# Four transformer layers on one core: the order and the queues of the first loads

## The chip, the cores and the metric

One Trainium2 chip, one core of it. The metric is the device time of one execution in microseconds (us). Profiles are one execution each, of the same programs; times in them count from the start of the span, which is about 1.8 us shorter than the device time.

## The reference

Input 2048 x 1024 in bf16; linear attention and a gated feed-forward layer, each with a layernorm ahead and a residual, two times over. Only the beginning matters here:

```python
x = A_x                                                        # 1 x 2048 x 1024
x = x + _A_ref(_layernorm(x, axis=-1), A_wqkv, A_wo)           # linear attention
x = x + _B_ref(_layernorm(x, axis=-1), B_W_gate, B_W_up, B_W_down)
...  # both once more
def _A_ref(x, wqkv, wo):
    q, k, v = ...(x @ wqkv)
    ...
```

Nothing can be multiplied before the first rows of x are loaded, normalized and transposed, and the first weights are there.

## The kernel before

Rows of x come in 16 blocks of 128 rows (256 KB each); weights in tiles of 1024 x 512 (1 MB). `k0`, `k1`, `q0`, `q1`, `v0` are such tiles of `wqkv`. The first four blocks make the first quarter. TensorE is kept busy with multiplications of zeros until block 0 is ready, for its clock.

```python
        for _ in range(11):
            nc.tensor.matmul(idle, lhsT=zero[:, 0:P], rhs=zero, start=True, stop=True)

        k0, k1, v0, q0, q1 = (ring.place() for _ in range(5))
        self.load_x(0, 0)                     # half of block 0, SyncE's queue
        self.load_x(0, 1, nc.scalar)          # other half, ScalarE's queue
        k0(0, H)
        self.load_x(1, None, nc.scalar)
        k0(H, 2 * H)
        self.load_x(2)
        k1()
        self.load_x(3)

        def load():
            for t in range(4, 8):
                self.load_x(t)
            q1()
            ...  # blocks 8 to 15 and v0, spread over later units
```

Then the units of work, in the order in which every engine gets them. A unit is the projection of one block with one weight tile: eight matmuls of 512 columns, 1.73 us at full clock.

```python
        def block0():
            stat(0, 0)
            stat(0, 1)
            rstd(0)
            stat(1, 0)                        # block 1's statistics, ahead of the scaling of block 0
            scale(0, 0)
            scale(0, 1)
            t0 = turn(0, 0)                   # transposes on TensorE
            t1 = turn(0, 1)
            t0("ss")
            stat(1, 1)
            rstd(1)
            q0(0, 2 * H, self.nc.scalar)      # query weights, ScalarE's queue
            t1("v")
            k(0, 0, between)
        ...
        return ([block0, block1, lambda: (turned(2), norm(3), k(0, 1)),
                 lambda: (turned(3), load(), k(1, 1)), lambda: q(0, 0), lambda: q(1, 0)]
                + ...)                        # k(2,0), k(2,1), q(2,0), k(3,0), ...
```

So the order on TensorE is k0 on blocks 0 and 1, k1 on blocks 0 and 1, then q0 on blocks 0 and 1. Blocks 2 and 3 are transposed by DMA on SyncE's queue.

Of the kernel before, what the change touches and what calls it, by code (L numbers as in the profile page):

```python
# [80 lines left out]
class _Net:  # L81
# [131 lines left out]
    def head(self):  # L213

        nc, tc, ring = self.nc, self.tc, self.ring
        H = self.KT // 2

        zero = self.ep.tile([P, NW], BF16, tag="e")
        nc.vector.memset(zero, 0.0)
        idle = self.ps3.tile([P, NW], F32, tag="b")  # L220
        for _ in range(11):
            nc.tensor.matmul(idle, lhsT=zero[:, 0:P], rhs=zero, start=True, stop=True)

        k0, k1, v0, q0, q1 = (ring.place() for _ in range(5))
        self.load_x(0, 0)
        self.load_x(0, 1, nc.scalar)
        k0(0, H)
        self.load_x(1, None, nc.scalar)
        k0(H, 2 * H)
        self.load_x(2)  # L230
        k1()
        self.load_x(3)

        def load():
            for t in range(4, 8):
                self.load_x(t)
            q1()
            for t in range(8, self.ST):
                self.later.at(3 + (t - 8) // 2 * 2, lambda t=t: self.load_x(t))
            self.later.at(11, v0)  # L240

        src = self.xb
        self.xnT[0, 0] = self.xnTp.tile([P, self.KT, QT * P], BF16, tag="xnT", name="xnT0_0")
        stats = [self.small.tile([P, 2, nc.vector.BN_STATS_DIM], F32, tag="stats", name=f"st{j}")
                 for j in range(QT)]
        rs, xn = {}, {}

        def stat(j, c):
            self.ln_stat(j, src[j], c, stats[j])

        def rstd(j):
            rs[j] = self.ln_rstd(stats[j])
            xn[j] = self.xn_home(0, j)

        def scale(j, h=None):
            self.ln_scale(src[j], *rs[j], xn[j], h)

        def turn(j, h):
            tp = self.ps3.tile([P, H, P], BF16, tag="b")
            for i in range(H):  # L260
                kt = h * H + i
                nc.tensor.transpose(tp[:, i, :], xn[j][:, kt * P:(kt + 1) * P], self.ident)  # L262
            dst = self.xnT[0, 0][:, h * H:(h + 1) * H, j * P:(j + 1) * P]

            def take(engine):
                if engine == "v":
                    nc.vector.tensor_copy(out=dst, in_=tp)
                elif engine == "s":
                    nc.scalar.activation(out=dst, in_=tp, func=ACT.Copy)
                else:  # L270
                    for i in range(0, H, 2):
                        nc.scalar.activation(out=dst[:, i:i + 2, :], in_=tp[:, i:i + 2, :],  # L272
                                             func=ACT.Copy)

            return take

        return load, q0, H, xn, stat, rstd, scale, turn

    def head_units(self, k, q, load, q0, H, xn, stat, rstd, scale, turn):

        def block0():
            stat(0, 0)
            stat(0, 1)
            rstd(0)
            stat(1, 0)
            scale(0, 0)
            scale(0, 1)
            t0 = turn(0, 0)
            t1 = turn(0, 1)
            t0("ss")  # L290
            stat(1, 1)
            rstd(1)
            q0(0, 2 * H, self.nc.scalar)
            t1("v")
            k(0, 0, between)

        def between():

            scale(1, 0)
            t0 = turn(1, 0)  # L300
            scale(1, 1)
            t0("v")

        def block1():
            turn(1, 1)("v")
            norm(2)
            k(1, 0)

        def norm(j):
            stat(j, 0)  # L310
            stat(j, 1)
            rstd(j)

        def turned(n):
            scale(n)
            self.ln_turn(0, n, xn[n])

        return ([block0, block1, lambda: (turned(2), norm(3), k(0, 1)),
                 lambda: (turned(3), load(), k(1, 1)), lambda: q(0, 0), lambda: q(1, 0)]
                + [lambda f=f, j=j, c=c: f(j, c) for j in (2, 3) for f, c in ((k, 0), (k, 1), (q, 0))]  # L320
                + [lambda j=j: q(j, 1) for j in range(QT)])
# [422 lines left out]
```

## Time and profile before

| what | us |
|---|---|
| median of 3 runs (lowest, highest) | 1627.52 (1626.98, 1627.64) |
| span of the profiled run | 1625.4 |
| TensorE busy | 1613.2 |
| first projection matmul starts | 7.49 |
| first query projection starts | 14.94 |
| last matmul of the program starts | 1622.12 |

The last two are starts of single matmuls in the trace. In the profile, "busy" of TensorE includes the matmuls' modelled ends, so a busy TensorE can still have lost some tenths of a us between two starts: the pauses below are taken from the distance of two starts, less the 0.216 us that is regular for 512 columns. The prediction shows the lines.

### The profile page before, as it was taken

How to read it: one execution, taken by the hardware profiler on the slowest of the kernel's cores; microseconds unless marked ns; L12 is line 12 of the kernel's file. 1: busy time of each engine (PE TensorE's matmuls, PEld its weight loads, DVE VectorE, ACT ScalarE, POOL GpSimd, SP SyncE). 2: the span in 40 equal slices, each digit the busy share in tenths (PEclk: the TensorE clock that was granted, in tenths of full speed). 3: DMA queues.
4: the chain of work that ended last, by engine and by line, in shares of the span. 5: the costliest groups of instructions: out<-in, count | busy, mean ns of one | idle time of the engine just before them, and what ended most of it. 6: DMA issues, size and time to landing. Idle time of an engine off the chain costs nothing.

```text
span 1625.4 us, 18607 instructions
## 1 busy us (share of the span) xinstructions
PE 1613.2 (99%) x7605; PEld 739.4 (45%) x7739; DVE 567.7 (35%) x940; ACT 330.4 (20%) x635; POOL 202.1 (12%) x134
## 2 busy tenths in 40 slices
PE   9999999999999999999999999999999999999999
PEld 4444444444444444444444444444444444444444
DVE  8844694113212222222264447932021112111211
ACT  6741212101110210111067312121011101101110
POOL 1449220000000000000023582100000000000000
PEclk9999999999999999999999999999999999999999
DMA  9314547447455545544550157464654455454442
GB/s 269 55 52 66 172 79 203 146 158 215 156 162 195 156 147 165 160 154 139 166 111 1 54 107 240 86 189 145 193 161 152 154 178 155 146 170 150 155 162 71
DMA packets 300358, 235.58 MB, mean 145 GB/s; under 512 B 103408, under 2 KB 296304, under 8 KB 300272
## 3 DMA queue, kind: packets, MB, share of 16 engines
q1 hardware_dynamic: 294192, 228.75, 48.3%
q10 hardware_dynamic: 6080, 5.64, 1.0%
q8 instruction: 60, 0.98, 0.3%
q14 instruction: 26, 0.21, 0.0%
HBM read 201.33 MB, written 8.39 MB: 129 GB/s over the span
## 4 chain that ended last, share of the span: by engine, by line
PE 99%; issue 0%; DMA 0%; DVE 0%; ACT 0%
PE pu L643 24%; PE pg L643 24%; PE acc L667 23%; PE ps L410 14%; PE ps L536 7%; PE ps L445 7%; PE kv L458 0%; PE acc_last L667 0%; DMA x<-in_A_x_dram 0%; PE fold L521 0%; PE tp L262 0%; PE ps L435 0%; ACT L692 0%; DVE xo L684 0%; DVE x L156 0%
## 5 line engine op out<-in xcount | busy, mean ns | idle before, releaser
L643 PEld LDWEIGHTS <-t 128*128 128x128 bf16 x3584 | 350.7, 98 | 422.8
L643 PE MATMUL pu<-xnT,t 128*128 128x512 bf16 x1756 | 420.1, 379 | 2.0
L643 PE MATMUL pg<-xnT,t 128*128 128x512 bf16 x1756 | 419.8, 379 | 1.8
L667 PE MATMUL acc<-t,hT 128*128 128x512 bf16 x1728 | 380.6, 379 | 1.9
L649 DVE TENSOR_TENSOR hT<-pu,rg 128x512 bf16<-128x512 f32 x224 | 154.8, 691 | 571.5 <-PE pu L643 555.0
L648 ACT ACTIVATE rg<-pg 128x512 f32<-128x512 f32 x224 | 133.5, 596 | 736.1 <-PE pg L643 661.7
L667 PEld LDWEIGHTS <-hT 128*128 128x128 bf16 x1820 | 178.1, 98 | 209.0
L410 PE MATMUL ps<-t,xnT 128*128 128x512 bf16 x1024 | 223.4, 379 | 0.2 <-ACT xnT L272 0.2
L410 PEld LDWEIGHTS <-xnT 128*128 128x128 bf16 x1024 | 99.4, 98 | 120.0 <-issue 1.5
L536 PE MATMUL ps<-T,pqT 128*128 128x512 bf16 x500 | 110.2, 379 | 0.6
L147 ACT ACTIVATE rstd<-mv,eps 128x1 f32<-128x1 f32 x64 | 18.8, 294 | 337.7 <-DVE mv L145 337.5
L684 DVE TENSOR_TENSOR xo<-x,acc 128x512 bf16<-128x512 f32 x31 | 21.3, 687 | 170.3 <-PE acc L667 169.5
L489 POOL TENSOR_TENSOR prod<-pq,zrow 128x1024 f32<-128x1024 bf16 x32 | 68.0, 2125 | 85.9 <-DVE den L494 72.4
L140 DVE BATCH_NORM_STATS2 stats<-x 128x6 f32<-128x512 f32 (+1 forms) x120 | 77.9, 671 | 1.2 <-DMA x<-in_A_x_dram 0.4
L536 PEld LDWEIGHTS <-pqT 128*128 128x128 bf16 x512 | 49.9, 98 | 60.4 <-issue 0.5
L425 POOL CAST ksum<-x 128x512 f32<-128x512 bf16 x2 | 1.7, 866 | 605.4 <-DVE x L361 605.4
L681 DVE TENSOR_TENSOR x<-x,acc 128x512 f32<-128x512 f32 x32 | 21.6, 674 | 138.5 <-PE acc L667 137.4
L427 POOL TENSOR_TENSOR ksum<-ksum,slab 128x512 f32<-128x512 f32 x46 | 54.1, 1183 | 80.3 <-DVE slab L361 63.0
L361 DVE SCALAR_TENSOR_TENSOR pq<-ps,e 128x512 bf16<-128x512 f32 x64 | 43.9, 686 | 53.3 <-ACT e L355 51.3
L501 POOL TENSOR_TENSOR pq<-pq,den 128x1024 bf16<-128x1024 bf16 x32 | 61.7, 1936 | 3.1 <-DVE den L496 3.1
L494 DVE TENSOR_REDUCE den<-prod 128x32 f32<-128x1024 f32 x32 | 38.9, 1217 | 54.0 <-POOL prod L489 54.0
L445 PE MATMUL ps<-slab,x 128*128 128x512 bf16 x249 | 55.7, 379 | 0.4
(57 smaller groups left out, 592.5 us busy)
## 6 DMA issues: line engine op xcount, KB each, us to landing
t<-in_B_W_gate_dram SPq DMA_DIRECT2D x56, 1024.0 KB, 7.3
t<-in_B_W_up_dram SPq DMA_DIRECT2D x56, 1024.0 KB, 5.4
t<-in_B_W_down_dram SPq DMA_DIRECT2D x64, 896.0 KB, 5.1
t<-in_A_wqkv_dram SPq DMA_DIRECT2D x10, 1024.0 KB, 5.1
t<-in_A_wo_dram SPq DMA_DIRECT2D x4, 1024.0 KB, 6.7
away<-x SPq DMA_DIRECT2D x8, 512.0 KB, 4.7
x<-away SPq DMA_DIRECT2D x8, 512.0 KB, 8.2
out_dram<-xo ACTq DMA_DIRECT2D x31, 128.0 KB, 2.5
```

Source lines behind the costliest of these rows:

```text
L140: self.nc.vector.bn_stats(out=stats[:, c, :], in_=src[:, c * fmax:(c + 1) * fmax])
L361: nc.vector.scalar_tensor_tensor(out=out, in0=ps, scalar=0.0, in1=e, op0=ALU.max, op1=ALU.add)
L410: nc.tensor.matmul(by_row(ps), lhsT=self.xnT[l, l_q][:, kt, j * P:(j + 1) * P], rhs=w[:, kt, :].rearrange("p (b i d) -> p i b d", i=R, d=H ...
L427: nc.gpsimd.tensor_tensor(out=ksum[:, cols], in0=ksum[:, cols], in1=pk, op=ALU.add)
L445: nc.tensor.matmul(ps, lhsT=self.xn[l, t][:, d * P:(d + 1) * P], rhs=self.pk[l, t][:, h * NW:(h + 1) * NW], start=(t == 0), stop=(t == sel ...
L489: nc.gpsimd.tensor_tensor(out=prod, in0=pq_of[sc, j], in1=zrow, op=ALU.mult)
L501: nc.gpsimd.tensor_tensor(out=heads(pq), in0=heads(pq), in1=den[:, :].unsqueeze(2).to_broadcast([P, D // HD, HD]), op=ALU.mult)
L536: nc.tensor.matmul(ps, lhsT=pqT[sc][:, g, j * P:(j + 1) * P], rhs=T[g // 2][:, g % 2, n2 * NW:(n2 + 1) * NW], start=(g == 0), stop=(g == G ...
L643: nc.tensor.matmul(ps, lhsT=w[:, kt, fi * P:(fi + 1) * P], rhs=self.xnT[l, q][:, kt, :], start=(kt == 0), stop=(kt == KT - 1))
L648: nc.scalar.activation(out=rg, in_=pg, func=ACT.Relu)
L649: nc.vector.tensor_tensor(out=h[:, fi, :], in0=pu, in1=rg, op=ALU.mult)
L667: nc.tensor.matmul(ps[:, 0:n], lhsT=hT[ft // 4][:, ft % 4, j * P:(j + 1) * P], rhs=wd[:, k, i * n:(i + 1) * n], start=(ft == 0), stop=(ft ...
```

## The change

Its intent: let block 0 arrive alone and sooner (both halves on SyncE's queue; block 1 on ScalarE's, held back by a tiny write to its buffer that has to come first), load all key weights ahead of blocks 2 and 3, and send the first query weights from SyncE in the same order, instead of from ScalarE in the middle of its work. One idle matmul goes.

```diff
-        for _ in range(11):
+        for _ in range(10):
             nc.tensor.matmul(idle, lhsT=zero[:, 0:P], rhs=zero, start=True, stop=True)
...
         self.load_x(0, 0)
-        self.load_x(0, 1, nc.scalar)
+        self.load_x(0, 1)
+
+        nc.vector.memset(self.xb[1][:, 0:2], 0.0)
+        self.load_x(1, None, nc.scalar)
         k0(0, H)
-        self.load_x(1, None, nc.scalar)
         k0(H, 2 * H)
+        k1()
         self.load_x(2)
-        k1()
         self.load_x(3)
+        q0()
...
             rstd(1)
-            q0(0, 2 * H, self.nc.scalar)
             t1("v")
```

More of the change, by code (lines that the diff above doesn't have):

```diff
@@ L275, in turn, with head_units @@
             return take
-        return load, q0, H, xn, stat, rstd, scale, turn
-    def head_units(self, k, q, load, q0, H, xn, stat, rstd, scale, turn):
+        return load, xn, stat, rstd, scale, turn
+    def head_units(self, k, q, load, xn, stat, rstd, scale, turn):
         def block0():
```

## The prediction

> **What bounds the kernel now.** I read the page's busy shares and chain first, then the chain of the first 60 us, the timeline of the first 20 us, the waits of the first 60 us, the DMA issues in narrow windows, and the stretches of 1 us with their DMA columns. The page:
>
> ```profile
> PE 1613.2 (99%) x7605; PEld 739.4 (45%) x7739; DVE 567.7 (35%) x940; ACT 330.4 (20%) x635; POOL 202.1 (12%) x134
> PE 99%; issue 0%; DMA 0%; DVE 0%; ACT 0%
> ```
>
> TensorE is busy for 1613 of 1625 us and carries 99% of the chain that ended last. All that is not matmul on it is some 12 us, and the change touches only the start. So what can be won or lost is what lies before TensorE runs without gaps. The chain of the first 60 us, and in the timeline what its places are:
>
> ```profile
> 1.19 4.34 DMA x<-in_A_x_dram
> 5.55 0.03 DVE st L140
> 6.16 0.41 DVE x L156
> 7.05 0.39 ACT xnT L272
> 7.49 1.47 PE ps L410 x6
> 9.85 50.36 PE ps L410 x233
> ...
> 1.34 4.67 PE L222 MATMUL idle<-zero 128*128 128x512 bf16 x11 [1.34 <-DVE zero L219]
> 3.78 1.29 DVE L140 BATCH_NORM_STATS2 st<-x 128x6 f32<-128x512 bf16 x2 [2.49 <-DMA x<-in_A_x_dram]
> 5.55 0.69 DVE L140 BATCH_NORM_STATS2 st<-x 128x6 f32<-128x512 bf16 x1 [0.24 <-DMA x<-in_A_x_dram]
> 6.62 0.72 PE L262 MATMUL tp<-ident,x 128*128 128x128 bf16 x8 [0.60 <-DVE x L156]
> ```
>
> First column: start; second: duration; in the brackets the idle time before it and who ended it. The start of the real work hangs on two landings: block 0 (statistics from 3.78) and block 1, which lands at 5.53 and whose first statistics stand on VectorE ahead of the scaling of block 0 (6.16). The scaling releases the transposes (6.62), these the copy (7.05), this the first projection (7.49). From 9.85 the chain is projections alone.
>
> The second set shows what comes after, from the timeline of TensorE's weight loads and the stretches (columns: stretch, us, busy of PE with count, PEld, DVE, ACT, POOL, granted clock, DMA share, GB/s):
>
> ```profile
> 14.94 5.06 PEld L410 LDWEIGHTS <-xnT 128*128 128x128 bf16 x24 [0.16 <-issue]
> 8.09 0.39 ACTq L36 DMA_DIRECT2D t<-in_A_wqkv_dram  x1
> ...
> 3.00:4.00 1.00, 1.00 (x4) 0.42 (x3) 0.22 (x1) 0.00 (x0) 0.00 (x0) 1.00 1.06 383
> 9.00:10.00 1.00, 1.00 (x12) 0.61 (x10) 0.60 (x3) 0.34 (x1) 0.00 (x0) 1.00 1.09 348
> 13.00:14.00 1.00, 1.00 (x6) 0.45 (x5) 1.00 (x2) 0.00 (x0) 0.00 (x0) 1.00 1.01 323
> ...
> t<-in_A_wqkv_dram ACTq DMA_DIRECT2D x1, 1024.0 KB, 6.8
> ```
>
> The first query weights are issued at 8.09 and land 6.8 us later, at 14.9; the first query projection (fifth of the 1.73 us projection units) starts at 14.94. The small pause of 0.16 us says that TensorE and this landing arrive together. And from 3 to 14 us the 16 DMA engines are full (share 1.01 to 1.10).
>
> **The Trainium skill.** "DMA: Bandwidth & Descriptors", section "Issuing engines are not separate DMA queues": transfers of ScalarE and SyncE run on the same 16 engines and interleave; a second issuer saves issue time only. The trace agrees: with both queues or one, the rate is 350 to 385 GB/s. Its section "Queues, rings and completion order" says that an engine takes turns between the queues that have work, so a split x block shares with the key weights: in 3.5 to 4.5 us both queues moved data, in 5 to 10.5 only SyncE's. "TensorE: Matmul & The Clock Gate", "What's actually happening": full clock only after about one free-running window of 3.4 us of sustained work. The idle matmuls start every 0.427 us (weight loads at 1.75, 2.17, 2.60), later ones of the same shape every 0.216 us; the trace's clock record rises at 5.68 us. The column for granted clock shows 1.00 even in the slow part, so I go by the spacing. "Perfetto Trace Analysis", "DMA Instruction — HWDGE (DVE, Sync)": the issue's duration leaves out the data movement; so I use landings only.
>
> **The change part by part.** The instruction orders of the two builds differ, on all five engines, only in these places: one idle matmul fewer, one 128x1 write on VectorE more, and the DMA issues moved.
>
> 1. One idle matmul less: TensorE's warming ends at 5.59 instead of 6.01. The transposes came at 6.62, so this alone gains 0; it only removes a floor, for transposes that come before 6.0.
>
> 2. Block 0 on SyncE alone, block 1 held. The write on VectorE follows the clearing of the idle operand (1.01 + 0.27), so ScalarE issues block 1 at about 1.4 instead of 1.19; its data starts about 1.5 us later (on this queue the first packet of the issue at 0.76 came at 2.28). Until 2.9 block 0 has the engines alone. Before, 14 of 16 engines delivered its first half by 3.58 and the last two at 3.76, while sharing; alone I estimate 3.4, the second half 3.7. The path from landing to scaling, from the timeline: statistics of both halves to 5.10, aggregate, two ScalarE steps to 5.87: 2.15 us after the 3.74 of the landing. From 3.4 it is 5.55. Block 1 lands at about 2.9 + 1.5 (256 KB at half of 350 GB/s) + 0.6 from last packet to landing = 5.0; its statistics hold the scaling for 0.61 more: 5.65. So scaling begins at about 5.7 instead of 6.16: 0.45 us won here (0.1 to 0.65), and all the following steps (transposes 6.15, projection 7.05) move with it.
>
> 3. Do the key weights keep up? Bytes in order times the rate of the stretches: 0.22 MB by 3.0, then 383, 386, 364, 349, 373, 350, 348, 365, 358, 349, 323 KB per us. Up to the second half of the first key weights 1.57 MB must be moved, before as after: 6.6, and landings lag this by 0.95 (second key weights before: 2.88 MB are reached at 10.3, landing 2.75 + 8.5 = 11.25). So 7.6; the fifth projection matmul wants it at 8.36 - 0.45 = 7.9. It fits by 0.3. The second key weights, now ahead of block 2, need 2.62 MB: 9.55 + 0.95 = 10.5 instead of 11.25; wanted at 11.0. The 0.2 us weight-load wait before them disappears, but the matmul spacing there showed no gap, so it gains 0.
>
> 4. First query weights behind all that, on the same queue. The sum of everything ahead and including them is 4 x 256 + 3 x 1024 KB = 4.19 MB, exactly as before. The stretches add up to 4.17 MB at 14.0. So their last packets come at about 14.05 whatever the queue, landing 14.7 to 14.9. TensorE would now want them at 14.94 - 0.45 = 14.5. It waits 0.2 to 0.4 us there. The won 0.45 us is given back up to what the landing itself gains. I give this 0.15 us (the transposes of block 2 ran into its last packets at 14.2 and do not any more); with the 0.04 us of matmul spacing lost at 14.94 (0.254 against 0.216) that makes about 0.2 us.
>
> 5. Blocks 2 and 3 later. Block 2 now ends at 2.88 MB: 10.3 + 0.95 = 11.25 instead of 2.20 + 6.1 = 8.3. VectorE wanted it at 10.23: its statistics, scaling and the joins behind them move by 1.0 us. Its transpose on SyncE's queue, before 12.92 + 3.1 = 16.0, ends at about 17; its projection starts near 18.3. PSUM: the first join ends at 15.35 + 1.0, the bank is wanted again at 18.3. The second query weights, behind in SyncE's order, go from 19.16 + 8.0 = 27.2 to 28.2; wanted at 28.8 (twelve units of 1.73 after about 8). All hidden, the last by only 0.6.
>
> Sum: 0 + 0.45 won at the start, 0.25 lost again at the query weights, 0 elsewhere: -0.2 us of 1627.5, or 0.01%: 1627.3.
>
> **The rivals.** (a) The gain stays: the query weights land early enough, say at 14.5, and the whole 0.45 to 0.65 us arrives at the end: 1626.9 to 1627.0. For it: the queue changes hands less, and the issue no longer waits for ScalarE at 8.09. Against: the engines have no empty stretch that could be filled. (b) A new wait: the shift of block 2 on VectorE, or of the second query weights, reaches TensorE: 0.2 to 0.8 us more, 1627.7 to 1628.3. For it: 0.6 us of slack after a shift of 1.0. Against: VectorE has idle places up to 21 us that take up part of it. (c) The clock rises later, because ten idle matmuls end at 5.59 and the window is not full: work up to 9 us at half rate costs about 1.3 us, of which the wait for the query weights absorbs half. Against: up to 5.68 only 0.1 of 3.4 us would be empty. (d) Block 1, held, lands later than before (issue 1.4 + 4.3 = 5.7): then scaling starts at 6.3, nothing is won, and 0.2 us of loss is hidden or not: 1627.5.
>
> **Range and chances.** The centre is 1627.3. Three runs of before spread over 0.66 us, which is more than the effect. (a) at 25%, (b) 15%, (c) 5% give the tails: 1626.6 to 1628.0. No part of this can reach 2% (32 us): the whole start, until projections run without a gap, is 9.85 us. Within 2%: 0.99.
>
> **What would show it.** Block 0's statistics start near 3.4 and scaling near 5.7 (step 2); no weight-load wait for the second key weights (3); a pause of 0.2 to 0.4 us before the first query projection, still at 14.7 to 14.9 (4); block 2's statistics near 11.25, no new pause of TensorE after 15 us (5). Wrong would be: the query projection starting at 14.5 or earlier without a pause, or a gap near 18.3 or 28.8, or idle matmuls' spacing carried into the projections.

## The result, and the profile after

Median 1627.76 us (1627.34 to 1628.62, 6 runs) against 1627.70 us (1626.98 to 1628.43, 6 runs). The ratio is 1.0001, 95% interval 0.9988 to 1.0014: the same. (A ratio is the mean time of one kernel's runs over that of the other's of the same rounds, so it is not quite the ratio of the medians.) The time lies in the predicted range; the predicted gain of 0.2 us is not there. All 11 runs of the changed kernel have a mean of 1628.01, the 33 of the kernel before that ran beside them 1627.40, so if there is a difference, it is a loss of some 0.6 us, or 0.04%. Most of it comes from the second measurement (means 1628.21 against 1627.36); in the six rounds of the first the means differ by 0.14. No interval separates that from none; the traces can say where tenths of a us go, as they repeat to 0.01 us where nothing waits.

The profiled execution took 1628.05 us, that of before 1627.18. The page after:

```profile
PE 1620.4 (100%) x7738; PEld 739.2 (45%) x7738; DVE 567.9 (35%) x941; ACT 329.8 (20%) x635; POOL 202.1 (12%) x134
PE 97%; DVE 1%; DMA 1%; SPq 0%; ACT 0%; issue 0%; DVEq 0%
```

TensorE is still all that counts, but 1% of the chain each has gone to VectorE and DMA. (The trace has 133 matmul records more than that of before, of the same program less one matmul; records can be missing, so the 7 us more of busy time say nothing.) From the chain of the first 60 us (start, duration, what):

```profile
5.31 10.15 DMA t<-in_A_wqkv_dram
15.50 10.54 PE ps L412 x48
26.03 0.67 DVE slab L363
...
54.84 0.60 DVE pq L363
55.49 4.69 PE ps L412 x21
```

Two things are new: TensorE starts from the landing of the query weights, 10.15 us after their issue, and between 26 and 55 us the chain runs through VectorE. The timeline of the changed kernel:

```profile
1.34 4.45 PE L222 MATMUL idle<-zero 128*128 128x512 bf16 x10 [1.34 <-DVE x L228]
2.91 0.69 DVE L140 BATCH_NORM_STATS2 st<-x 128x6 f32<-128x512 bf16 x1 [1.61 <-DMA x<-in_A_x_dram]
4.53 0.69 DVE L140 BATCH_NORM_STATS2 st<-x 128x6 f32<-128x512 bf16 x1 [0.93 <-DMA x<-in_A_x_dram]
6.54 0.72 PE L265 MATMUL tp<-ident,x 128*128 128x128 bf16 x8 [0.74 <-DVE x L156]
7.41 1.47 PE L412 MATMUL ps<-t,xnT 128*128 128x512 bf16 x6 [0.15 <-ACT xnT L275]
11.87 1.29 DVE L140 BATCH_NORM_STATS2 st<-x 128x6 f32<-128x512 bf16 x2 [1.64 <-DMA x<-in_A_x_dram]
15.50 5.77 PE L412 MATMUL ps<-t,xnT 128*128 128x512 bf16 x26 [0.51 <-DMA t<-in_A_wqkv_dram]
```

The first half of block 0 is there at 2.9, 0.9 us earlier than before, but the second half at 4.5. So the first projection comes at 7.41, only 0.08 us earlier. The query projection comes at 15.50, 0.56 us later than before (14.94). The weight loads near 55 us in the same timeline:

```profile
55.49 1.60 PEld L412 LDWEIGHTS <-xnT 128*128 128x128 bf16 x8 [0.40 <-issue]
```

And three stretches of 1 us, one early and two at the end of the query weights (columns as in the prediction; the last is GB/s):

```profile
3.00:4.00 1.00, 1.00 (x4) 0.42 (x3) 0.60 (x1) 0.00 (x0) 0.00 (x0) 1.00 0.89 292
13.00:14.00 1.00, 1.00 (x7) 0.43 (x5) 0.37 (x2) 0.53 (x3) 0.00 (x0) 1.00 1.07 341
14.00:15.00 1.00, 0.98 (x5) 0.35 (x4) 1.00 (x2) 0.45 (x1) 0.00 (x0) 1.00 0.23 72
```

At 55.49 TensorE lost 0.28 us (0.50 between two starts). From 14 to 15 us only 72 GB/s were moved, before the query weights were complete at 15.46: most of the 16 DMA engines had nothing left to do. The records of landing, 16 per load, which I read as one per engine, say why: 15 shares had landed by 14.89, the last one at 15.46. The same pattern, the last share behind the 15th, is seen in the second half of block 0 (3.73 and 4.51), not in the first half of the key weights (5.97 and 6.10), and from their second half on: 7.54 and 8.18; second key weights 10.58 and 11.17. From 3 to 4 us the rate was 292 GB/s, where it had been 383; step 3 below comes back to this.

The sum for the two profiled runs: +0.56 at the query projection, +0.28 near 55 and +0.04 near 62 us make 0.88; the last matmul starts 0.88 us later (1622.99 against 1622.12), the execution was 0.87 us longer. So nothing else happened in the other 1560 us.

### The profile page after: what moved, and what is told of

Same layout as the page of the kernel before. It is cut to its first block, busy times and chain, and to the rows that moved or that the text cites. A ratio compares the mean times of both kernels' runs of the same rounds, so it can differ in the third digit from the quotient of the medians.

```text
span 1626.3 us, 18740 instructions
## 1 busy us (share of the span) xinstructions
PE 1620.4 (100%) x7738; PEld 739.2 (45%) x7738; DVE 567.9 (35%) x941; ACT 329.8 (20%) x635; POOL 202.1 (12%) x134
## 4 chain that ended last, share of the span: by engine, by line
PE 97%; DVE 1%; DMA 1%; SPq 0%; ACT 0%; issue 0%; DVEq 0%
PE pu L645 24%; PE pg L645 24%; PE acc L669 23%; PE ps L412 11%; PE ps L538 7%; PE ps L447 7%; DMA t<-in_A_wqkv_dram 1%; PE kv L460 0%; DVE stats L140 0%; PE acc_last L669 0%; DVE pq L363 0%; DVE slab L363 0%; DVE e L361 0%; PE fold L523 0%; SPq L374 0%
## 5 line engine op out<-in xcount | busy, mean ns | idle before, releaser
L147 ACT ACTIVATE rstd<-mv,eps 128x1 f32<-128x1 f32 x64 | 18.8, 294 | 344.2 <-DVE mv L145 344.1
```

## The experiments

The first rivals: the late query weights and the pause at 55 us belong to the changed kernel, or they are an accident of that one execution. Then: which part of the change makes them. Twelve runs were made (two of them repeats of a kernel), all correct, each with a trace and five timed rounds, four to a chip. This table has the readings; below, each kernel with what had been expected. "k0" is the landing of the second half of the first key weights, first and last of the 16 engines. "scaling" is the first scaling of block 0. "gap" is the start of the last matmul of the program less the start of the first query projection.

| kernel | mean of runs (median) | scaling | k0 landed | query projection | gap |
|---|---|---|---|---|---|
| before, first trace | 1627.40 (1627.33), 33 runs | 6.16 | 6.88 to 7.59 | 14.94 | 1607.18 |
| changed, first trace | 1628.01 (1627.98), 11 runs | 6.07 | 7.10 to 8.18 | 15.50 | 1607.49 |
| changed again | (among the 11) | 5.19 | 6.90 to 8.22 | 15.53 | 1607.39 |
| start only | 1627.49 (1627.52) | 5.48 | 6.96 to 8.13 | 15.48 | 1607.17 |
| order only | 1627.71 (1627.53) | 5.88 | 6.91 to 7.99 | 15.31 | 1607.17 |
| block 2 first | 1627.74 (1627.86) | 5.11 | 6.97 to 8.28 | 15.65 | 1607.17 |
| before again | 1627.34 (1627.43) | 5.99 | 6.96 to 7.84 | 15.20 | 1607.17 |
| block 3 behind | 1629.08 (1628.74) | 5.48 | 7.11 to 7.73 | 14.94 | 1609.30 |
| not held | 1628.98 (1628.76) | 6.18 | 7.17 to 9.04 | 16.53 | 1607.18 |
| block 4 ahead | 1628.20 (1628.20) | 5.12 | 6.88 to 7.67 | 15.94 | 1607.18 |
| not held, eleven idle | 1628.65 (1628.69) | 6.04 | 7.03 to 9.02 | 16.30 | 1607.57 |
| block 3 mended | 1627.36 (1627.25) | 5.45 | 7.12 to 8.26 | 15.48 | 1607.18 |
| changed, eleven idle | 1627.83 (1627.78) | 5.34 | 7.07 to 7.94 | 15.27 | 1607.45 |
| before, ten idle | 1627.06 (1627.07) | 5.87 | 7.01 to 7.31 | 14.81 | 1607.18 |

Read the last column first. In nine of the 14 traces the rest of the program takes 1607.17 or 1607.18 us from the first query projection on, whatever came before. In the other five the excess is pauses that the trace shows. And each profiled execution took 5.05 to 5.09 us more than the start of its last matmul, so the traces account for the times. So the moment of the first query projection is the time of the head, and what happens before it does not matter unless it moves it.

On the landings: in start only, block 2 first and before again nearly all shares of the query weights are recorded as landed together (15.34 to 15.43 in start only). There the packets tell more: in all 14 traces the last 1 KB packet of the weights ends 0.46 to 0.65 us before the last landing (14.89 in start only), so the engine that works longest still sets it. No transfer of the instruction queue lies between 0.1 and 19 us in any trace, so that is not what holds an engine up at the start.

**The changed kernel again.** No edit.

> The changed kernel once more. In its first trace the first query projection started at 15.50 us (14.94 before), after a pause of 0.51 us, because one of 16 DMA engines landed its share 0.6 us after the other 15, and TensorE paused 0.28 us at 55.5 because VectorE was 1.65 us behind. Theory 1 (bytes in order): these are the kernel's own: again a pause of 0.3 to 0.6 us at 14.9 to 15.5, again one near 55, time 0.3 to 0.9 us over before. Theory 2 (chance of one execution): the late engine is an accident; the first query projection now starts at 14.7 to 14.9 and the time is within 0.3 us of before.

Measured: 1628.51 median (1627.26 to 1628.76); ratio 1.0005, interval 0.9993 to 1.0018. Query projection at 15.53, a pause of 0.18 at 55.4. Theory 1 holds in the place, theory 2 does not. But the start is quite different this time. TensorE:

```profile
5.66 0.97 PE L265 MATMUL tp<-ident,x 128*128 128x128 bf16 x8
6.74 1.04 PE L412 MATMUL ps<-t,xnT 128*128 128x512 bf16 x4
8.26 0.59 PE L412 MATMUL ps<-t,xnT 128*128 128x512 bf16 x2 [0.49 <-DMA t<-in_A_wqkv_dram]
...
15.53 44.80 PE L412 MATMUL ps<-t,xnT 128*128 128x512 bf16 x206 [0.58 <-DMA t<-in_A_wqkv_dram]
```

Both halves of block 0 were there by 3.63, scaling began at 5.19 and the first projection at 6.74: 0.75 us before the kernel before. TensorE then waited for the second half of the first key weights, and again for the query weights, and came out at 15.53, as in the execution whose start had won nothing. The gain at the start is real, and all of it is given back.

**Start only.**

```diff
 (against the changed kernel)
-        k1()
         self.load_x(2)
+        k1()
         self.load_x(3)
-        q0()
...
             rstd(1)
+            q0(0, 8, self.nc.scalar)
```

> Only the start of the change: block 0 on SyncE's queue, block 1 held on ScalarE's, ten idle matmuls; block 2 ahead of the second key weights and the query weights from ScalarE at 8.1, as before. Theory 1: scaling of block 0 between 5.7 and 6.1, the first query projection at 14.9 with a pause of what was won (0.1 to 0.4 us), no pause near 55, time within 0.2 us of before. If instead the late DMA engine comes from this start (block 0 on one queue), its second half lands at 4.4 or later here too and the query projection starts near 15.5.

Measured: ratio 1.0001 (0.9988 to 1.0013). Scaling at 5.48, query projection at 15.48, no pause near 55. The start alone wins 0.66 us at the first projection (6.83) and loses it in three waits for weights: 0.47 us at 8.17, 0.62 at 11.86, 0.15 at 15.48. I had expected a single wait, at 14.9.

**Order only.**

```diff
 (against the kernel before)
-        self.load_x(2)
         k1()
+        self.load_x(2)
         self.load_x(3)
+        q0()
...
-            q0(0, 2 * H, self.nc.scalar)
```

> Only the order of the change: second key weights ahead of block 2, query weights on SyncE's queue behind block 3; the start (block 0 split over both queues, block 1 not held, eleven idle matmuls) as before. Theory 1: scaling at 6.16 as before, statistics of block 2 at 11.2 to 11.9, no pause or below 0.1 us at the query projection (14.9), a pause of about 0.2 to 0.3 us near 55 from VectorE; time 0.2 to 0.4 us over before. If the shift of block 2 is hidden, as I had predicted: no pause after 15 us and time equal to before.

Measured: ratio 1.0002 (0.9990 to 1.0015). Statistics of block 2 at 11.68 as expected, but the query projection at 15.31 after a pause of 0.69, and no pause near 55. So the late query weights do not come from the new start only; here too one engine is late from the second half of the key weights on (7.28 and 7.99). And a late block 2 does not suffice for the pause near 55.

**Block 2 first.**

```diff
 (against the changed kernel)
-        k1()
         self.load_x(2)
+        k1()
         self.load_x(3)
         q0()
```

> The changed kernel with block 2 put back ahead of the second key weights. Its bytes come before the key weights', 2.88 MB before these land: 10.3 + 0.95 = 11.2 or, with the late engine, 11.8, where 11.2 is wanted. If the pause at 55 us comes from the late block 2, it is gone here, statistics of block 2 at 10.2, and the time is 0.3 us under the changed kernel; the query projection as in the changed kernel.

Measured: ratio 1.0002 (0.9989 to 1.0016). The pause near 55 is gone and statistics of block 2 are at 10.17, as expected; but the time is 0.27 us under the changed kernel (means 1627.74 and 1628.01), near the 0.3 expected and less than the spread of the runs; the query projection was at 15.65 in this trace.

What makes the pause near 55 can be read by comparing traces. Timeline of VectorE, statistics of block 4, first in the changed kernel, then in order only, then in the kernel before:

```profile
23.48 1.29 DVE L140 BATCH_NORM_STATS2 stats<-x 128x6 f32<-128x512 bf16 x2 [1.46 <-DMA x<-in_A_x_dram]
```

```profile
22.36 1.29 DVE L140 BATCH_NORM_STATS2 stats<-x 128x6 f32<-128x512 bf16 x2 [0.52 <-DMA x<-in_A_x_dram]
```

```profile
20.81 1.29 DVE L140 BATCH_NORM_STATS2 stats<-x 128x6 f32<-128x512 bf16 x2 [0.45 <-DMA x<-in_A_x_dram]
```

Block 2 late makes VectorE late, this makes the DMA transposes late, and these stand ahead of block 4 in SyncE's order (issued at 18.8 instead of 17.1). That is 1.7 us; in the changed kernel VectorE waits 1 us more for block 4, and this it has not made up at 55 us. The three traces with a pause there (changed twice, changed with eleven idle matmuls) are the three with 1.36 us or more in this wait (0.58 at most in the others). In these three an issue on SyncE amid the blocks 4 to 7 took 1.8 us instead of 0.43, at the time of a 16 KB transfer of the instruction queue; that this transfer delays block 4 is a guess that I did not test. It fits the trace of before, where the same transfer runs from 20.19 to 21.08: block 4 is whole at 20.79, and it is block 5 whose last share is late (21.36, then 22.78).

**Before again.** No edit.

> The kernel before once more, for a second trace. In its first trace the last engine brought the query weights at 14.90 us and TensorE began with them at 14.94. In all five traces of kernels with parts of the change one DMA engine is 0.4 to 0.8 us behind and this start is at 15.31 to 15.65. If the late engine is an accident of an execution, it can be here too: start at 14.9 to 15.6 and the end of the last matmul 1607.2 us after it. If the split start protects from it, 14.9 again. The ratio to before must be 1.000 within 0.0004: it shows what these timings can tell apart.

Measured: ratio 1.0000 (0.9987 to 1.0012). Query projection at 15.20 after waits of 0.27 for the second key weights and 0.17 for the query weights, which the first trace did not have. So the 14.94 of the first trace was a good one, and the differences from engine to engine are in the kernel before too. The interval shows what a comparison of two equal kernels can exclude here: nothing under 0.1%.

**Block 3 behind.**

```diff
 (against the changed kernel)
-        k1()
         self.load_x(2)
-        self.load_x(3)
+        k1()
         q0()
+        self.load_x(3)
...
-        return ([block0, block1, lambda: (turned(2), norm(3), k(0, 1)),
-                 lambda: (turned(3), load(), k(1, 1)), lambda: q(0, 0), lambda: q(1, 0)]
+        return ([block0, block1, lambda: (turned(2), k(0, 1)),
+                 lambda: (load(), k(1, 1)), lambda: (norm(3), q(0, 0)),
+                 lambda: (turned(3), q(1, 0))]
```

> The changed kernel with block 2 ahead of the second key weights, block 3 behind the query weights, and block 3's norm a unit later. If the bytes ahead of the query weights set the end: 0.26 MB less, at 350 KB per us 0.72 us earlier; the first query projection starts at 14.2 to 14.9 instead of 15.3 to 15.6, no pause near 55, time 0.5 to 0.8 us below the changed kernel (about 1626.9 to 1627.1). If TensorE is then held by the second key weights (11.9) or the VectorE shift of block 3, the gain is below 0.3 us or a new pause appears between 18 and 30.

Measured: ratio 1.0011 (0.9998 to 1.0023), slower in all runs. The part under test came out: with 0.26 MB less ahead of them, the query weights landed 10.7 us after their issue, at 14.4 instead of 15.46, and their projection began at 14.94 without a pause, held only by the second key weights before. But block 3's transpose had been put behind blocks 4 to 7 and another weight tile:

```profile
11.48 12.26 PE L413 MATMUL ps<-t,xnT 128*128 128x512 bf16 x56 [0.47 <-DMA t<-in_A_wqkv_dram]
25.68 34.49 PE L413 MATMUL ps<-t,xnT 128*128 128x512 bf16 x159 [1.95 <-DMA xnT<-x]
```

TensorE waited 2.1 us for it at 25.7: a mistake of mine in the edit, and the whole of the 1609.30 in the table.

**Not held.**

```diff
 (against the changed kernel)
-        nc.vector.memset(self.xb[1][:, 0:2], 0.0)
```

> The changed kernel without the write that holds block 1. Block 1 is issued at 0.76 instead of 1.34 and shares with block 0: block 0 lands 0.2 to 0.5 us later (first half 3.2 to 3.4), block 1 at about 4.3; the scaling starts at 5.3 to 5.8. If only the bytes ahead of the query weights count, their projection starts at 15.3 to 15.6 as in the changed kernel, and the time is the same within 0.2 us: the hold is worth nothing at the end.

Measured: 1628.76 median, ratio 1.0010 (0.9997 to 1.0024), the slowest start of all: query projection at 16.53. I had expected no difference at the end. Block 0's first half landed at 4.03, not at 3.2 to 3.4, and the scaling began at 6.18, not at 5.3 to 5.8. Two things are seen in its trace. The clock stayed low, as weight loads 0.43 us apart show, from 7.74 to 10.28; and the engines' shares of the first key weights landed from 7.17 to 9.04, a spread of 1.9 us.

```profile
1.35 4.45 PE L222 MATMUL idle<-zero 128*128 128x512 bf16 x10 [1.35 <-DVE zero L219]
6.65 1.04 PE L264 MATMUL tp<-ident,x 128*128 128x128 bf16 x8 [0.86 <-DVE x L156]
7.74 2.74 PE L411 MATMUL ps<-t,xnT 128*128 128x512 bf16 x6
```

Six matmuls took 2.74 us where they take 1.47 at full clock. Is this the missing idle matmul? That was tried next, below.

**Block 4 ahead.** One more x block ahead of the query weights.

```diff
 (against the changed kernel)
         self.load_x(3)
+        self.load_x(4)
         q0()
...
-            for t in range(4, 8):
+            for t in range(5, 8):
```

> The changed kernel with one more x block (256 KB) loaded ahead of the query weights. If the bytes ahead set the end, their projection starts 0.72 us later than in the changed kernel (16.1 to 16.4) and the time grows by 0.5 to 0.8 us, to about 1628.5. If something else holds TensorE (VectorE's backlog), the time stays.

Measured: ratio 1.0005 (0.9993 to 1.0018). Query projection at 15.94, 0.45 us later than in the changed kernel, instead of 0.72; the mean time, 1628.20, is 0.2 us above it, where I had expected 0.5 to 0.8. In this trace the last engine is less late (key weights by 7.67 instead of 8.18), which may be the difference. TensorE paused 1.67 us there, having arrived early; the lead of 1.03 us at the first projection (6.46 against 7.49) is gone all the same:

```profile
9.05 5.39 PE L413 MATMUL ps<-t,xnT 128*128 128x512 bf16 x24
15.94 44.41 PE L413 MATMUL ps<-t,xnT 128*128 128x512 bf16 x205 [1.51 <-DMA t<-in_A_wqkv_dram]
```

Block 2 was as late as in the changed kernel (11.46), block 4 was not, and there is no pause near 55. This fits the reading given above.

**Not held, eleven idle matmuls.**

```diff
 (against not held)
-        for _ in range(10):
+        for _ in range(11):
```

> The kernel without the hold, with eleven idle matmuls instead of ten. Without the hold and with ten, the trace showed half clock until 10.6 us (idle matmuls over at 5.79, transposes at 6.65) and 1628.76 us. If the missing idle matmul did this, the clock now rises at or before 7.2, matmuls after 7.5 are 0.216 us apart, and the time falls by about 1 us to 1627.3 to 1627.9. If sharing block 0 with block 1 did it, the time stays at 1628.3 or more.

Measured: 1628.69 median, ratio 1.0008 (0.9995 to 1.0021). The clock rose at 6.12 and matmuls came 0.216 us apart, but the time stayed. So the low clock was not what made the kernel slow: TensorE at full clock only waits longer for the same weights (0.81 us at 9.07, 0.71 at 16.30). The spread of the engines is there again (7.03 to 9.02). Two traces and ten runs of 1628.1 and more: with block 0 on one queue and block 1 unheld on the other, the last engine is 0.8 us later than in the changed kernel (9.0 against 8.2). Why, I did not find out. It also paused 0.39 us at 30.50 for the second query weights, the place that I had called the tightest in the prediction.

**Block 3 mended.**

```diff
 (against block 3 behind)
-        for _ in range(10):
+        for _ in range(11):
...
-        def load():
-            for t in range(4, 8):
-                self.load_x(t)
+        def load(rest=False):
+            if not rest:
+                for t in range(4, 8):
+                    self.load_x(t)
+                return
             q1()
...
-                 lambda: (turned(3), q(1, 0))]
+                 lambda: (turned(3), load(True), q(1, 0))]
```

> The kernel with block 3 behind the query weights, mended: eleven idle matmuls, and block 3's transpose ahead of the second query weights in SyncE's order (before it was behind them, and TensorE waited 1.9 us for it at 25.7). The first query projection starts at 14.7 to 15.0 as there; no pause above 0.2 us between 16 and 60. Then the time is 1627.0 to 1627.3: 0.5 to 0.9 under the changed kernel and 0 to 0.3 under before.

Measured: 1627.25 median against 1627.09 of before in the same rounds, ratio 1.0000 (0.9988 to 1.0013). The pause for block 3 is gone, and no other after 16 us. The query projection did not start at 14.9 but at 15.48, now held by the key weights, whose last engine was late again (8.26, and the second at 11.97): waits of 0.64 us at 8.30 and 0.64 at 12.01. This was to be a version that beats both. It does not beat the kernel before.

**Changed, eleven idle matmuls.**

```diff
 (against the changed kernel)
-        for _ in range(10):
+        for _ in range(11):
```

> The changed kernel with eleven idle matmuls. If ten are a risk for the clock in it too, the runs spread less (under 0.8 us instead of 1.5) and the median is 0.3 to 0.6 us lower, near 1627.5. If its excess comes from the late query weights and VectorE's backlog alone: first query projection at 15.3 to 15.6, a pause of 0.2 to 0.3 near 55, and the median stays at 1627.8 to 1628.3.

Measured: 1627.78 median (1627.44 to 1628.21), ratio 1.0003 (0.9989 to 1.0017). Query projection at 15.27, 0.24 us lost at 55.2. Second case of the expectation: the idle matmul is not the cause of the excess.

**Before, ten idle matmuls.**

```diff
 (against the kernel before)
-        for _ in range(11):
+        for _ in range(10):
```

> The kernel before with ten idle matmuls instead of eleven. My prediction gave the removal 0 us. If ten are a risk for the clock (its transposes come at 6.4 to 6.6, 0.6 to 0.8 us after the last idle one), some runs are 0.5 to 1.5 us slower: median 0.3 or more over before, highest above 1628.5. If not: within 0.2 us of before, spread as before's.

Measured: 1627.07 median (1626.99 to 1627.12), ratio 0.9998 (0.9986 to 1.0011). Nothing is lost by the removal, though the clock rose only at 7.27 here and the transposes still ran at half clock. In this trace all 16 engines landed within 0.3 us of one another (key weights 7.01 to 7.31), and it has the earliest query projection of all, 14.81. That ties the two together once more: first landings of these weights are 6.9 to 7.2 in all 14 traces, last ones 7.3 to 9.0.

## Why the prediction was right or wrong

The time was in the range and "the same" was right, and the main reason given holds: the start is followed by a stretch in which a fixed number of bytes has to arrive, so what the start wins is returned as a wait. The direction was wrong: a gain of 0.2 us was forecast, and both traces of the changed kernel lost. That the first median lay in the range is little proof, as the range is wider than every term of the sum; the second measurement's median, 1628.51, lies outside it. Step by step:

1. *One idle matmul less gains 0*: right. Before with ten, 1627.07 against 1627.09; changed with eleven, 1627.78 against the 1627.98 of all runs of the changed kernel. Rival (c), a late clock, did occur in one trace (not held, 10.6 us), and cost little, since the weights were later still.

2. *0.45 us won at the start*: the mechanism is right, the size is not one number. Scaling began at 6.07 in the first trace (0.09 us won) and at 5.19 in the second (0.97 won). The hold works as meant: first half of block 0 at 2.89 to 2.98 against my 3.4, block 1 at 4.29 to 4.70 against 5.0. In the first trace one engine brought the second half of block 0 at 4.51, where I had 3.7.

3. *The key weights keep up, "It fits by 0.3"*: wrong. The bytes in order were counted correctly, but I took their rate from the kernel before, and added the lag of one execution, 0.95 us, as if it were fixed. The last engine landed the second half of k0 at 8.2 where I had 7.6. Some 0.25 us of this is the rate: from 0 to 6.6 us the changed kernel moved 223 GB/s on average, the kernel before 236, so 1.57 MB were reached at 6.9 instead of 6.6. This goes with the new start: 206 to 232 GB/s in all ten traces that have it, 235 to 240 in the four that start as before (order only among them). Why was not tested. The rest is the longer lag of the last engine. When the start did win (changed again, start only, block 2 first), TensorE waited 0.47 to 0.65 us right here. The second key weights landed at 11.2 against my 10.5; TensorE lost nothing on them in the changed kernel, as said, since it was itself late.

4. *The query weights give the gain back; "I give this 0.15 us"*: this is the step that failed in size and sign. I expected the landing at 14.7 to 14.9 and a pause of 0.2 to 0.4. It was 15.46 and the pause 0.68 (second trace 15.5 and 0.74). The lag of 0.95 us from step 3, used here too, would have given 14.05 + 0.95 = 15.0 and no gain; the sum took a shorter one without a reason. The term that was mis-sized is the landing: -0.15 us in my sum, +0.56 measured in the first traces, and about +0.4 between the means of the two traces each (15.52 against 15.07). In the first traces the last engine makes it: 15 shares had landed by 14.88 before and by 14.89 after the change, and only 72 GB/s were moved from 14.0 on.

5. *Block 2 late, "All hidden"*: wrong. It cost 0.28 us at 55.5 in the first trace, 0.18 and 0.24 in two others. My shift of 1.0 us was 1.64 at block 2 (11.87 against 10.23) and 2.7 at block 4 (23.48 against 20.81). I had looked for trouble at 18 and 29 us and had counted on VectorE's idle places up to 21; the wait for block 4 took them away. This is rival (b), with 15% given to it; it came in all three traces of the changed kernel and its variant with eleven idle matmuls.

Rival (a), the gain stays, would have needed query weights at 14.5. None of the 14 traces shows a query projection before 14.81.

What is shown: where the time goes (the gap column), and that the landing of the weights, not the start, sets the query projection. How far the bytes ahead move it is shown less firmly: with 0.26 MB less the query weights landed at 14.4 and 14.9, with 0.26 MB more at 15.9, with the same bytes and the hold, or the start of before, at 14.7 to 15.6. That the last engine sets where in this stretch a trace falls is read from the landings; no experiment moved that engine alone. What stays open: why an engine falls behind (the last share of the second half of k0 lands 0.3 to 2.0 us after the first), why the new start moves fewer bytes at first, and whether the changed kernel's last engine is later than that of the kernel before. Three traces of before's start and order (ten or eleven idle) have 14.81 to 15.20, seven of kernels with the change or parts of it and the same bytes or less 15.27 to 15.65 (block 3 behind 14.94, the two not held 16.30 and 16.53); the means of the timed runs lean the same way, start only and block 3 mended hardly. That is a tendency in few traces, and the intervals do not exclude zero.

## What to carry to other kernels

When the DMA engines are full from the first us on, count the bytes ahead of each consumer and ask who is the first to wait for the end of the queue: here a lead of 0.3 us or more at the first projection was gone by the query projection in all eight traces that had one, and reordering the loads ahead of the query weights did not help. Add to the byte count the lag of the slowest of the 16 engines, and take that lag from several traces, since one trace may be a good one. And a load that is moved back on one engine's account moves every later load of an in-order queue; follow it until the slack is used up, not until the first consumer that still has some.

## What the Trainium skill lacked or had wrong

- "DMA: Bandwidth & Descriptors", section "Issuing engines are not separate DMA queues", says that a second issuer saves issue time only. It has nothing on the moment at which the second queue's load starts, and that mattered here: both kernels use the same two queues, but with block 1 sent at once on ScalarE's instead of held, the 16 shares of the following 512 KB load landed over 1.9 to 2.0 us (0.6 to 1.3 in the eight traces with the hold), and the means were 1628.65 and 1628.98 us against 1628.01. Two traces; the cause was not found.
- No page has a size for how far the engines of one load come apart. Over 14 traces the last share of the second half of the first key weights landed 0.3 to 2.0 us after the first share, with the first nearly constant (6.88 to 7.17).
- No page says how to read the clock before its first record. In the trace of before that record is at 5.68 us; the profile's column for granted clock shows 1.00 ahead of it too, while matmuls start only every 0.427 us. The first record comes at 4.88 to 7.27 us in 12 traces and at 10.6 in one; one trace has none.
